# Attention with mixed heads and a dense block: two six-chunk first units, unread products on TensorE, and k and v loaded by head pair

## The chip, the cores and the metric

The kernel runs on one core of one Trainium2 chip. The metric is the device time of one execution in microseconds (us). A profile is one execution taken by the hardware profiler; its span is the time from the first to the last instruction.

## What is computed

Attention over 4 batches, 12 heads, 448 tokens and 64 columns a head, whose heads are mixed before and after the softmax, and behind it a dense block with a token mix of rank 32:

```
scores = scale * matmul(q, k^T)                     # per batch and head
scores = einsum('bhij,hg->bgij', scores, w_pre)     # mix the heads
attn   = softmax(scores, axis=-1)
attn   = einsum('bhij,hg->bgij', attn, w_post)      # mix them again
x      = matmul(attn, v), heads side by side        # (4, 448, 768)
u      = x + (x^T @ U @ V)^T                        # mix the tokens
out    = u + relu(u @ w_ch1) @ w_ch2                # 768 -> 3072 -> 768
```

## The kernel before

A chunk is ten tokens of a batch with all their twelve heads. The tokens of a batch are cut into units of 9 to 12 chunks (table `UNITS`, four units a batch), and each unit goes through the following steps; a step is an entry of a plan, with the engines that may run it, a rank, the steps it needs and the buffers it holds. `Plan.order` writes the order of all steps, engine by engine, from the ranks (table `RANK`) and its own costs. Each engine then runs its list strictly in that order.

- Scores (`qk`, L412 to L419): a head pair p of unit u. Four products of 64 (or 60) rows by 448 columns run beside each other in the four quarters of TensorE's array: two heads, each in two halves of the unit's rows (up to 124 with four leading zero rows). They fill one of four PSUM tiles (`bank`), which ScalarE (ACT) or VectorE (DVE) copies to SBUF (`qk_out`, L433).
- Relay (`relay`, L435 to L437): one DMA a head copies its rows into the tile `t` so that a chunk's token-head pairs lie on partitions. The destination has ten rows. There are twelve relays a unit, issued by SP, those of the first two units by SP or ACT (L454). `t` has two buffers, used by units in turn.
- Premix (`premix`, L457 to L463): two chunks at a time, product of `t` with `wpre`. It needs all twelve relays of its unit. Then the row maximum on DVE (`neg_max`, L469), two exponentials on ACT (`exp`, L474), a reciprocal, and on GpSimd (POOL) the scaled weights `wr` (L484).
- Postmix (`postmix`, L486 to L499): 28 small products; ACT or DVE copies them to the tile `a` (`post_out`).
- Attention times v (`av`, L530 to L547): two steps a unit, three head pairs each, which need the unit's last `post_out`. L539 is the main part, L547 the rest of 64 keys. The results are added up in `acc`, and behind a batch's last unit comes the token mix (`tp`, `t1`, `hp`).

SP issues almost all DMAs in one queue in order: k of a batch in four loads of one or two head pairs (`K_LOADS`), all held until the first premix of the preceding batch's last unit (L410); q of a unit in two loads; v of a batch in one load of 1536 KB (L528); the relays; and weights. Behind the attention, from about 360 us on, the dense block runs in products of 128 x 128 by 448 (L992, L1100), whose operands DVE, ACT and POOL split into two parts (steps `W`, `T`, `w`, `S`).

Of the kernel before, what the change touches and what calls it, by code (L numbers as in the profile page):

```python
# [8 lines left out]
F32 = mybir.dt.float32  # L9
# [12 lines left out]
UNITS = [[10, 12, 12, 11], [11, 12, 12, 10], [12, 12, 12, 9], [11, 12, 12, 10]]  # L22
NG = 4
NJ = 4
# [4 lines left out]
MC = 10  # L29
# [16 lines left out]
class Unit:  # L46


    def __init__(self, b, gi):
        self.b, self.gi, self.n = b, gi, UNITS[b][gi]  # L50
        self.i0 = MC * sum(UNITS[b][:gi])
        self.rows = MC * self.n
        self.tokens = min(S, self.i0 + self.rows) - self.i0

# [3 lines left out]
    e0=-73.073, estep=7.59, er=5.082, qk_lead=5.047, qk_step=0.838, av_off=4.137, av_step=0.959, post=4.408,  # L58
    kr=1.361, vr=0.943, qr=4.83, mx=0.636, ex=1.029, ep=2.968, po=2.763, qo=1.169, uv0=6, uvs=0.013, uv1=2.315,
    raw=5.531, k0=-13.837, kstep=0.705, m0=7.671, pu=1.842, ev=29.543, lead=14.83, t0=-3.828, ts=0.557,  # L60
    t1=2.012, ta=31.914, tb=3.276, dl=32.545, hl=13.674, out=3,
# [6 lines left out]

WEIGHT = {("POOL", "ACT"): 1.0, ("POOL", "DVE"): 3.221, ("DVE", "POOL"): 0.8, ("ACT", "DVE"): 1.3}
# [22 lines left out]
class Plan:  # L92
# [29 lines left out]
    def order(self):  # L122
# [10 lines left out]
        events, seq, now, wire, out, shared, landed = [], 0, 0, 0, [], 0, []  # L133
# [40 lines left out]
        while events:  # L174
# [28 lines left out]
            while moved:  # L203
                moved = False
                for e in free:
# [22 lines left out]
                    if e == "PE" and now - free[e] > 600:  # L228
                        cost += min(cost, 850)
# [22 lines left out]
def build(tc, q2, kt, vj, wpre_in, wpost_in, u_in, v_in, ident, w1j, w2, out, show=None):  # L252
# [115 lines left out]

    units = [Unit(b, gi) for b in range(B) for gi in range(NG)]
    nu = len(units)  # L370
    chunks, first = [], {}
# [9 lines left out]
    load("wpre0", lambda: wpre, wpre_in, -30)  # L381
    load("wpost", lambda: wpost, wpost_in, -12)
# [14 lines left out]
    K_LOADS = ((0, 1), (1, 1), (2, 2), (4, 2))  # L397
    K_AT = (0, 1, 2, 2, 4, 4)
# [798 lines left out]
```

## Time and profile before

| | us |
|---|---|
| median of 3 timed runs (lowest, highest) | 1050.91 (1049.37, 1052.29) |
| the profiled execution | 1047.36 |
| its span | 1045.5 |
| TensorE busy in the span | 1000.9 |
| VectorE, ScalarE, GpSimd busy | 786.8, 473.6, 357.4 |

The engines run beside each other, so only one of them can be full, and busy time is not yet time on the path to the end: a wait counts where it delays the engine that sets the end. "Granted clock" is TensorE's clock as a share of 2.4 GHz; 0.50 is 1.2 GHz. A line ends with the idle time of the engine before it and what ended it, in brackets.

### The profile page before, as it was taken

To read this page: it belongs to the slowest core of one execution; us is meant where nothing else is said; L and a number is where in the kernel's file an instruction comes from. 1 tells how busy PE (TensorE), PEld (TensorE's weight loads), DVE (VectorE), ACT (ScalarE), POOL (GpSimd) and SP (SyncE) were. 2 spreads that over 40 slices of the span, in tenths; PEclk is the share of its full clock that TensorE was granted. 3 is DMA by queue.
4 is the path that set the end of the run, shared out by engine and by line. 5 is a ranking of instruction groups with operands and counts; after the bars stand their busy time and mean duration, and the time that the engine had idled before them with its cause. 6 is when DMAs were issued, how large, how long until landed. Compare 5 with 4: busy or idle time off the path is not lost.

```text
span 1045.5 us, 28572 instructions
## 1 busy us (share of the span) xinstructions
PE 1000.9 (96%) x11908; PEld 840.0 (80%) x11908; DVE 786.8 (75%) x1183; ACT 473.6 (45%) x980; POOL 357.4 (34%) x457
## 2 busy tenths in 40 slices
PE   6899999999899997999999999999999999999998
PEld 2465666666556696898998999999999999999997
DVE  3474575577567788899999897895999999996223
ACT  2677677777777864543433333441333323430000
POOL 3121121112112686765655543450432423322000
PEclk8899999999999999999999999999999999999999
DMA  6764655566585324345444444686353454440023
GB/s 220 208 176 149 203 176 170 180 221 181 182 262 181 97 95 145 108 137 157 148 154 138 140 146 132 191 280 253 94 168 125 138 171 131 151 149 1 1 81 131
DMA packets 84481, 161.30 MB, mean 154 GB/s; under 512 B 8624, under 2 KB 68992, under 8 KB 83840
## 3 DMA queue, kind: packets, MB, share of 16 engines
q1 hardware_dynamic: 82912, 157.11, 46.8%
q10 hardware_dynamic: 1440, 2.37, 0.7%
q8 instruction: 94, 1.54, 0.6%
q14 instruction: 35, 0.29, 0.1%
HBM read 86.13 MB, written 34.60 MB: 115 GB/s over the span
## 4 chain that ended last, share of the span: by engine, by line
PE 77%; DVE 12%; issue 5%; ACT 3%; DMA 2%; POOL 1%; SPq 0%; ACTq 0%; DVEq 0%; POOLq 0%
PE bank L1100 33%; PE bank L992 20%; PE bank L498 6%; PE bank L419 5%; PE bank L539 5%; PE bank L462 5%; DVE aw L686 2%; ACT e L474 1%; PE bank L547 1%; DVE aw L687 1%; DVE aw L682 1%; DVE w L341 1%; DVE x L691 1%; DVE st L469 1%; DVE x L692 1%
## 5 line engine op out<-in xcount | busy, mean ns | idle before, releaser
L1100 PE MATMUL bank<-u,w 128*128 128x448 f32 x1728 | 345.9, 362 | 0.0
L1100 PEld LDWEIGHTS bank<-u,w 128*128 128x128 f32 x1728 | 324.0, 187 | 21.6
L992 PE MATMUL bank<-u,w 128*128 128x448 f32 x1512 | 307.0, 363 | 4.8 <-DVE hs L1005 2.9
L992 PEld LDWEIGHTS bank<-u,w 128*128 128x128 f32 x1512 | 283.6, 188 | 26.1 <-ACT bank L334 2.6
L1103 DVE TENSOR_TENSOR acc<-acc,bank 128x896 f32<-128x896 f32 (+1 forms) x99 | 104.2, 1053 | 78.6 <-PE bank L1100 75.9
L696 POOL TENSOR_TENSOR aw<-aw,x 128x384 f32<-128x384 f32 x74 | 83.8, 1132 | 201.1 <-DVE x L692 197.4
L498 PEld LDWEIGHTS bank<-wr,e 60*64 60x64 f32 x5040 | 92.4, 136 | 52.4 <-issue 33.7
L469 DVE TENSOR_REDUCE st<-bank 128x2 f32<-128x896 f32 x90 | 97.4, 1086 | 45.6 <-PE bank L462 35.6
L474 ACT ACTIVATE e<-bank,st 128x448 f32<-128x448 f32 x180 | 113.0, 639 | 24.7 <-DVE st L469 9.8
L341 POOL TENSOR_TENSOR w<-aw,w 128x384 fp32r<-128x384 f32 x84 | 97.7, 1171 | 67.5 <-ACT w L334 66.0
L334 ACT CAST w<-aw 128x384 fp32r<-128x384 f32 x103 | 52.4, 515 | 134.9 <-PE bank L1100 65.9
L498 PE MATMUL bank<-wr,e 60*64 60x60 f32 x5040 | 95.7, 221 | 14.3 <-issue 9.3
L675 ACT ACTIVATE x<-kr 128x384 f32<-128x384 f32 (+1 forms) x80 | 44.3, 554 | 133.6 <-DMA kr<-in_w 101.2
L419 PE MATMUL bank<-k,q 64*64 64x448 f32 (+1 forms) x768 | 93.4, 569 | 8.0 <-DMA k<-in_kt 5.0
L462 PE MATMUL bank<-t,wpre 64*64 64x448 f32 x720 | 89.5, 569 | 6.4 <-DMA t<-acc 4.8
L477 POOL TENSOR_SCALAR st<-st 128x2 f32<-128x2 f32 x90 | 18.6, 206 | 205.2 <-ACT e L474 203.7
L334 ACT COPY hs<-bank 128x448 f32<-128x448 f32 x88 | 46.9, 533 | 76.2 <-PE bank L992 74.9
L1060 DVE SCALAR_TENSOR_TENSOR u<-hs,u 128x448 fp32r<-128x448 f32 x96 | 73.9, 800 | 0.0
L687 DVE SCALAR_TENSOR_TENSOR aw<-x,aw 128x384 f32<-128x384 f32 x88 | 67.3, 765 | 6.7
L334 ACT COPY a<-bank 128x840 f32<-128x840 f32 (+1 forms) x64 | 54.5, 854 | 34.6 <-PE bank L498 34.2
L692 DVE SCALAR_TENSOR_TENSOR x<-kr,x 128x384 f32<-128x384 uint32 (+2 forms) x99 | 66.8, 675 | 3.4
L334 ACT COPY s<-bank 124x896 f32<-124x896 f32 x64 | 58.1, 912 | 20.6 <-PE bank L419 14.5
(69 smaller groups left out, 1016.6 us busy)
## 6 DMA issues: line engine op xcount, KB each, us to landing
hd<-hs SPq DMA_DIRECT2D x96, 224.0 KB
hs<-hd SPq DMA_DIRECT2D x96, 224.0 KB
t<-s SPq DMA_DIRECT2D x99, 210.0 KB
kr<-in_w1j SPq DMA_DIRECT2D x48, 384.0 KB
kr<-in_w SPq DMA_DIRECT2D x48, 384.0 KB
t<-s SPq DMA_DIRECT2D x36, 192.5 KB
v<-in_vj SPq DMA_DIRECT2D x4, 1536.0 KB
q<-in_q SPq DMA_DIRECT2D x32, 186.0 KB
```

Source lines behind the costliest of these rows:

```text
L334: eng.copy(out=o, in_=i)
L341: eng.tensor_tensor(out=o, in0=a, in1=b, op=ALU.subtract)
L419: eng.matmul(o[at, i, :S], lhsT=q[d, p, at], rhs=k[d, p, :], start=True, stop=True)
L462: eng.matmul(o[64 * j:64 * j + 64, i, :S], lhsT=wpre[64 * i:min(64 * i + 64, QW)], rhs=tt[u % 2][64 * i:min(64 * i + 64, QW), n, :], start ...
L469: eng.tensor_reduce(out=mx, in_=T["pre", k][:, :, :S], axis=AX.X, op=ALU.max, negate=True)
L474: eng.activation(out=e[:, i], in_=T["pre", k][:, i, :S], func=ACTF.Exp, bias=T["mx", k][:, i:i + 1], accum_out=sm[:, i:i + 1])
L498: eng.matmul(d, lhsT=e[64 * j:64 * j + HALF, i, x * KB:x * KB + KB], rhs=wr[64 * j:64 * j + HALF, i].rearrange("p (g m) -> p g m", m=MH), ...
L687: eng.scalar_tensor_tensor(out=f32(a), in0=f32(x), scalar=MIN_NORMAL, in1=f32(a), op0=ALU.is_ge, op1=ALU.mult)
L696: eng.tensor_tensor(out=f32(a), in0=f32(a), in1=f32(x), op=ALU.add)
L992: eng.matmul(o, lhsT=w[:, x, i * 128:(i + 1) * 128], rhs=u[:, i, y, :], start=j < 2 and i + t == 0, stop=i + t == 4, skip_group_check=True)
L1100: eng.matmul(ps[:, j, :S], lhsT=w[:, x, cc * 128:(cc + 1) * 128], rhs=h, start=(i == 0), stop=(i == len(todo) - 1))
L1103: eng.tensor_tensor(out=two(b, c, n), in0=two(b, c, n), in1=T.pop(("dn", g, b, c))[:, :n, :S], op=ADD)
```

## The change

Batch 0 is cut into five units of 6, 6, 12, 12 and 9 chunks. A unit of six chunks has at most 64 rows with its zero rows, so one `qk` step takes two head pairs, one in each half of the array's columns; its copy has 128 rows, and it is followed by four relays of six chunks. The relays of the first unit alone may be issued by ACT. TensorE gets two steps `warm`, three and five products of a zeroed tile into a PSUM tile that nobody reads, the second behind the scores of both small units. The k of batch 0 comes in three loads of two head pairs, that of the others in six of one, held from some twenty chunks ahead of the batch; v comes in six loads. The planner's own cost for a cold TensorE and the ranks are changed, which moves steps on all engines.

```diff
-UNITS = [[10, 12, 12, 11], [11, 12, 12, 10], [12, 12, 12, 9], [11, 12, 12, 10]]
+UNITS = [[6, 6, 12, 12, 9], [11, 12, 12, 10], [12, 12, 12, 9], [11, 12, 12, 10]]
...
+        self.pairs = 2 if self.rows + QA <= 64 else 1
+        self.cols = 64 if self.pairs == 2 else QW
...
-    e0=-73.073, estep=7.59, er=5.082, qk_lead=5.047, qk_step=0.838, av_off=4.137, av_step=0.959, post=4.408,
+    e0=-97.289, estep=7.59, er=4.323, qk_lead=4.915, qk_step=0.84, av_off=3.794, av_step=0.935, post=4.408,
...
+SHARED = 1
+WARM = 3, 5
...
-    K_LOADS = ((0, 1), (1, 1), (2, 2), (4, 2))
-    K_AT = (0, 1, 2, 2, 4, 4)
+    K_LOADS = ((0, 2), (2, 2), (4, 2)), tuple((p, 1) for p in range(H // 2))
+    Q_LOADS = ((0, 2), (2, 4)), ((0, 6),), ((0, 3), (3, 3))
...
     for b in range(B):
-        for p, n in K_LOADS:
-            plan.add(("k", b, p), [("SP", (450, 650 * n))], partial(load_k, b=b, p=p, n=n), rank_qk(b * NG, 2 * p) - RANK["kr"], [("premix", first[b * NG - 1] // 2)] if b else (), [("k", b)])
+        start = first[of_batch[b][0]]
+        for p, n in K_LOADS[b > 0]:
+            plan.add(("k", b, p), [("SP", (450, 650 * n))], partial(load_k, b=b, p=p, n=n), rank_qk(of_batch[b][0], 2 * p) - RANK["kr"], [("premix", (start - 20 + p) // 2)] if b else (), [("k", b)])
...
         for j in range(2):
-            at = slice(64 * j, min(64 * j + 64, QW))
+            at = of = slice(64 * j, min(64 * j + 64, QW))
+            pj = p
+            if units[u].pairs == 2:
+                at, of, pj = slice(64 * j, 64 * j + 64), slice(0, 64), p + j
             for i in range(2):
                 d = slice(i * D, (i + 1) * D)
-                eng.matmul(o[at, i, :S], lhsT=q[d, p, at], rhs=k[d, p, :], start=True, stop=True)
+                eng.matmul(o[at, i, :S], lhsT=q[d, pj, of], rhs=k[d, pj, :], start=True, stop=True)
...
-                plan.add(("relay", u, h), [("SP", cost)] + [("ACT", cost)] * (u < 2), partial(relay, u=u, h=h), r + RANK["qo"], [("qk_out", u, p)], s + [("t", u)])
+                plan.add(("relay", u, h), [("SP", cost)] + [("ACT", cost)] * (u < SHARED), partial(relay, u=u, h=h), r + RANK["qo"], [("qk_out", u, p)], s + [("t", u)])
...
+    def blank():
+        return sb["xn"].tile([JP, NJ, LW], F32R, "xh", ("xn", "blank")).bitcast(F32).rearrange("p j n -> p (j n)")
+
+    def warm(eng, i, n):
+        z, o = blank(), bank("pre", ("warm", i))
+        for _ in range(n):
+            eng.matmul(o[:64, 0, :S], lhsT=z[:, S:S + 64], rhs=z[:, :S], start=True, stop=True)
+
+    plan.add("blank", [("DVE", 700)], lambda eng: eng.memset(blank(), 0.0), -30, (), [("xn", "blank")])
+    for i, n in enumerate(WARM):
+        plan.add(("warm", i), [("PE", 760 * n)], partial(warm, i=i, n=n), (-30, -1)[i], ["blank"] + [[], [("qk", 1, 4), ("qk", 0, 4)]][i], [("pre", ("warm", i)), ("xn", "blank")])
...
-            plan.add(("v", un.b), [("SP", (500, 3900))], partial(load_v, b=un.b), rank_av(u, 0) - RANK["vr"], [("premix", first[u] // 2)], [("vr", un.b)])
+            for p in range(H // 2):
+                plan.add(("v", un.b, p), [("SP", (450, 650))], partial(load_v, b=un.b, p=p), rank_av(u, p // AV * AV) - RANK["vr"], [("premix", (max(first[u], first[u + 1] - 6) + p) // 2)], [("vr", un.b)])
```

The order of three places follows, first before and then after. A row is a line of the program, the operation, what it writes and reads, its shape and a count; L419 and L435 are scores, L462 and L495 premixes, L498 and L531 postmixes, L437 and L456 relays.

**TensorE, from the last scores of the second unit to the first postmix** (bank0 to bank3 are the PSUM tiles, q_1 and q_2 the q of the second and third unit):

```order
L419 MATMUL bank3_61<-k_0_151,q_1_159 64x448 x2
L419 MATMUL bank3_61<-k_0_151,q_1_159 60x448 x2
L462 MATMUL bank0_58<-t0_142,wpre_141 64x448 x4
L462 MATMUL bank1_59<-t0_142,wpre_141 64x448 x4
L462 MATMUL bank2_60<-t0_142,wpre_141 64x448 x4
L462 MATMUL bank3_61<-t0_142,wpre_141 64x448 x4
L498 MATMUL bank0_58<-wr_0_284,e_0_270 64x12x5 x24
```

```order
L484 MATMUL bank0_58<-xh_0_149 64x448 x3
L435 MATMUL bank1_59<-k_0_153,q_0_147 64x448 x4
L435 MATMUL bank2_60<-k_0_153,q_0_147 64x448 x4
L435 MATMUL bank3_61<-k_0_153,q_0_147 64x448 x4
L435 MATMUL bank0_58<-k_0_153,q_1_158 64x448 x4
L435 MATMUL bank1_59<-k_0_153,q_1_158 64x448 x4
L435 MATMUL bank2_60<-k_0_153,q_1_158 64x448 x4
L484 MATMUL bank3_61<-xh_0_149 64x448 x5
L495 MATMUL bank0_58<-t1_143,wpre_141 64x448 x4
L495 MATMUL bank1_59<-t1_143,wpre_141 64x448 x4
L495 MATMUL bank2_60<-t1_143,wpre_141 64x448 x4
L435 MATMUL bank3_61<-k_0_153,q_2_230 64x448 x2
```

Before, twelve score steps and four premixes stand ahead of the first postmix; now it is three unread products, six score steps, five unread products, three premixes and two score steps of the third unit, of which the first row is shown.

**SP, its first DMAs** (in_q, in_kt are inputs in DRAM; t_142 and t_143 the two relay buffers; acc and s the copies of the scores):

```order
L379 DMA wpre<-in_wpre 124x64
L406 DMA q_149<-in_q 128x372
L402 DMA k_151<-in_kt 128x448
...
L402 DMA k_151<-in_kt 128x896
L379 DMA wpost<-in_wpost 128x60
...
L406 DMA q_159<-in_q 128x372 x2
L437 DMA t_142<-acc 10x10x448 x6
L437 DMA t_143<-acc 10x12x448 x3
L437 DMA t_143<-s_234 10x12x448
...
L406 DMA q_260<-in_q 128x372
...
L528 DMA v_282<-in_vj 128x3072
```

```order
L418 DMA q_147<-in_q 128x4x64
L414 DMA k_153<-in_kt 128x896
L418 DMA q_158<-in_q 128x6x64
...
L389 DMA wpre<-in_wpre 124x64
...
L389 DMA wpost<-in_wpost 128x60
L456 DMA t_143<-acc 10x6x448 x6
L456 DMA t_142<-acc 10x6x448 x7
L418 DMA q_230<-in_q 128x372 x2
L456 DMA t_142<-acc 10x6x448 x5
L561 DMA v_300<-in_vj 128x512
L456 DMA t_143<-acc 10x12x448 x6
```

Before, SP has half the relays of both first units; now it has six of the first and all twelve of the second, with the third unit's q between them, and one sixth of v ahead of the third unit's relays.

**TensorE, around the first scores of batch 1** (k_1128 and k_1012 are that batch's k):

```order
L462 MATMUL bank_60<-t_143,wpre 64x448 x4
L462 MATMUL bank_58<-t_143,wpre 64x448 x4
L462 MATMUL bank_59<-t_143,wpre 64x448 x4
L498 MATMUL bank_61<-wr_284,e_270 64x12x5 x24
...
L419 MATMUL bank_60<-k_1128,q_159 64x448 x2
...
L419 MATMUL bank_58<-k_1128,q_159 64x448 x2
```

```order
L435 MATMUL bank_58<-k_1012,q_230 64x448 x2
...
L495 MATMUL bank_61<-t_142,wpre 64x448 x4
L531 MATMUL bank_60<-wr_346,e_259 64x12x5 x24
...
L435 MATMUL bank_59<-k_1012,q_230 64x448 x2
...
L495 MATMUL bank_58<-t_142,wpre 64x448 x4
L435 MATMUL bank_60<-k_1012,q_230 64x448 x2
...
L531 MATMUL bank_59<-wr_256,e_239 64x12x5 x24
```

Before, three premixes in a row go ahead of the new batch's scores, three of which then follow each other with no premix between them; now scores, premixes and postmixes alternate.

## Rows read from the trace of the kernel before

**Rows 1.** The page's first part: TensorE's busy time, share of the span, instructions.

```profile
PE 1000.9 (96%) x11908; PEld 840.0 (80%) x11908; DVE 786.8 (75%) x1183; ACT 473.6 (45%) x980; POOL 357.4 (34%) x457
```

**Rows 2.** Stretches: length, each engine's busy time, granted clock, DMA share, GB/s.

```profile
5.00:9.00 4.00, 3.39 (x20) 0.71 (x16) 0.00 (x0) 1.31 (x2) 4.00 (x2) 1.00 0.95 311
12.00:20.00 8.00, 5.25 (x56) 1.59 (x48) 5.52 (x6) 2.72 (x3) 0.00 (x0) 1.00 0.64 217
22.00:23.00 1.00, 0.99 (x8) 0.53 (x12) 0.00 (x0) 0.00 (x0) 0.00 (x0) 0.50 0.64 220
85.60:89.00 3.40, 3.40 (x36) 1.38 (x40) 0.17 (x1) 1.79 (x3) 0.52 (x2) 0.50 0.24 70
400.00:420.00 20.00, 13.65 (x59) 11.02 (x58) 16.59 (x23) 9.06 (x19) 14.05 (x13) 0.91 0.43 143
```

**Rows 3.** TensorE in order of time: start, length, instructions, idle time before.

```profile
4.38 1.77 PE L419 MATMUL bank<-k,q 64*64 64x448 f32 x8 [4.38 <-DMA k<-in_kt]
...
22.01 5.98 PE L462 MATMUL bank<-t,wpre 64*64 64x448 f32 x32 [4.76 <-DMA t<-acc]
30.45 3.00 PE L498 MATMUL bank<-wr,e 60*64 60x60 f32 x112 [2.46 <-POOL wr L484]
...
39.97 0.69 PE L498 MATMUL bank<-wr,e 60*64 60x60 f32 x32 [2.56 <-issue]
...
85.51 3.21 PE L419 MATMUL bank<-k,q 64*64 64x448 f32 x16 [0.70 <-ACT e L474]
```

**Rows 4.** TensorE up to 45.36 us, by line: L419, L462, L498 (records in brackets).

```profile
0.00:45.36 45.36, 15.73 (x120) 0.85 0.71 216
...
0.00:45.36 45.36, 10.47 (x56) 0.85 0.71 216
...
0.00:45.36 45.36, 6.09 (x280) 0.85 0.71 216
```

**Rows 5.** TensorE in order of time at full clock: premix, postmix, scores.

```profile
57.60 0.93 PE L462 MATMUL bank<-t,wpre 64*64 64x448 f32 x8
58.35 0.99 PE L498 MATMUL bank<-wr,e 60*64 60x60 f32 x56
59.17 0.93 PE L419 MATMUL bank<-k,q 64*64 64x448 f32 x8
```

**Rows 6.** SP and ScalarE in order of time: first k, first relays, first exponential.

```profile
1.59 0.43 SPq L402 DMA_DIRECT2D k<-in_kt  x1
...
7.14 13.36 SPq L437 DMA_DIRECT2D t<-acc  x9
...
28.10 0.63 ACT L474 ACTIVATE e<-bank,st 128x448 f32<-128x448 f32 x1 [9.36 <-DMA t<-s]
```

**Rows 7.** Issue of relays on SP, ns (least/median/most): up to 30 us, then from 45.

```profile
L437 SPq DMA_DIRECT2D t<-acc x9: 755/1222/1555, 7.1 to 19.2; - x9
...
L437 SPq DMA_DIRECT2D t<-s x163: 755/756/1482, 45.0 to 346.9; - x163
```

**Rows 8.** Attention times v in order of time: units of 12 and of 9 chunks.

```profile
179.99 2.07 PE L539 MATMUL bank<-a,v 128*64 128x120 f32 x36
181.99 0.58 PE L547 MATMUL bank<-a,v 64*64 64x60 f32 x24
...
292.35 1.62 PE L539 MATMUL bank<-a,v 128*64 128x90 f32 x36 [0.56 <-DVE a L336]
293.89 0.56 PE L547 MATMUL bank<-a,v 64*64 64x45 f32 x24
```

**Rows 9.** Who TensorE waited for, 45 to 380 us: total, times, longest.

```profile
PE bank L498 <- issue: 6.8, 8, 1.4
PE bank L419 <- ACT e L474: 2.2, 5, 0.7
...
PE bank L462 <- ACT e L474: 0.6, 2, 0.4
...
PE bank L462 <- DMA t<-s: 0.5, 1, 0.5
```

More of the change, by code (lines that the diff above doesn't have):

```diff
@@ L132, in order @@
         ready = {e: [] for e in free}
-        events, seq, now, wire, out, shared, landed = [], 0, 0, 0, [], 0, []
+        events, seq, now, wire, out, shared, landed, cold = [], 0, 0, 0, [], 0, [], 4500
         def push(k, t):
@@ L367, in OUT, with side @@
         return [("ACT", 55 + 0.833 * n), ("DVE", 75 + 1.042 * n)]
-    units = [Unit(b, gi) for b in range(B) for gi in range(NG)]
+    units = [Unit(b, gi) for b in range(B) for gi in range(len(UNITS[b]))]
     nu = len(units)
+    of_batch = [[u for u in range(nu) if units[u].b == b] for b in range(B)]
+    def side(u):
+        return (nu - 1 - u) % 2 ^ 1
     chunks, first = [], {}
@@ L439, in build @@
+        r = QA + 64 * (h // 2 - p)
+        eng.dma_start(out=tt[side(u)][QA + h::H][:, :n], in_=T["s", u, p][r:r + MC * n, h % 2])
     at = 0
     for u, un in enumerate(units):
-        b, size = un.b, 128 * (H // 2) * QW
+        b, size = un.b, 128 * (H // 2) * un.cols
         src = q2[at:at + size].rearrange("(p h i) -> p h i", p=128, h=H // 2)
         at += size
-        for p in range(0, H // 2, 3):
-            plan.add(("q", u, p), [("SP", (430, 600))], partial(load_q, u=u, p=p, n=3, src=src), rank_qk(u, 2 * p) - RANK["qr"], [("premix", first[u - 2] // 2)] if u > 1 else (), [("q", u)])
@@ L446, in build @@
-        for p in range(H // 2):
+        at_q, hold = [], [("qk", 0, 4)] if u == 1 else []
+        for p, n in Q_LOADS[min(u, 2)]:
+            at_q += [p] * n
+            plan.add(("q", u, p), [("SP", (430, 200 * n * un.cols // QW))], partial(load_q, u=u, p=p, n=n, src=src), rank_qk(u, 2 * p) - RANK["qr"], [("premix", first[u - 2] // 2)] if u > 1 else (), [("q", u)])
+        for p in range(0, H // 2, un.pairs):
             r = rank_qk(u, 2 * p)
             o, s = ("qk", (u, p)), [("s", (u, p))] if lent(u, p) is None else []
-            plan.add(("qk", u, p), [("PE", 760)], partial(qk, u=u, p=p), r, [("q", u, p // 3 * 3), ("k", b, K_AT[p])],
+            plan.add(("qk", u, p), [("PE", 760)], partial(qk, u=u, p=p), r, [("q", u, at_q[p]), *hold, *{("k", b, x) for x in (([p // 2 * 2]) if b == 0 else range(p, p + 1))}],
@@ L794, in build @@
     for b in range(B):
-        RB = first[(b + 1) * NG] + RANK["uv0"]
-        us = range(b * NG, (b + 1) * NG)
+        us = of_batch[b]
+        RB = first[us[-1] + 1] + RANK["uv0"]
         for k in range(KC // 2):
@@ L1144, in lay_out @@
     for b in range(B):
-        for gi in range(NG):
+        for gi in range(len(UNITS[b])):
             un = Unit(b, gi)
-            part = np.zeros((2, D, H // 2, QW), q.dtype)
+            part = np.zeros((2, D, H // 2, un.cols), q.dtype)
             for n in range(un.n):
```

53 lines of the change are left out of this document (29 added, 24 removed).

## Prediction

> **What bounds the kernel now.** I read the page first: TensorE is busy for 1000.9 of 1045.5 us [rows 1], so a change can win only where TensorE waits or runs at the lower of its two clocks. Next came the stretches and TensorE's order in time. From about 45 us on it hardly stops; before that it does. The first scores start at 4.38 us, the first premix at 22.01, the first postmix at 30.45, and at 39.97 another wait of 2.56 us ends [rows 3]. The clock adds to it: granted 0.50 (1.2 GHz) at 22 us after the long wait [rows 2], and the very first head pair took 1.77 us where one takes 0.93 later [rows 3, 5], as at half clock, though the record reads 1.00 there [rows 2].
>
> How much is lost there? By 45.36 us TensorE had done 15 head pairs of scores (120 records of 8 a pair), 7 premixes (56 of 8) and 5 postmixes (280 of 56) [rows 4]. At full clock a premix starts 0.75 us before what follows it, a postmix 0.82, and a head pair lasts as long as a premix [rows 5]. That is 22 x 0.75 + 5 x 0.82 = 20.6 us of work in 45.4 us: **24.8 us lost**, the largest loss in the program.
>
> What sets it is the way of the scores: product, copy out of PSUM, relay by DMA into the layout the premix reads. A unit's premix needs all twelve relays. While relays alone move, the core moves 217 GB/s at a DMA share of 0.64; while the first loads move it is 311 GB/s at 0.95 [rows 2]. ScalarE's relays also hold up its exponentials: the first starts at 28.10, 9.36 us after ScalarE's last work, and 2.35 us before the first postmix [rows 6, 3].
>
> **The change, part by part.** *First premix.* A unit of six chunks has 60 rows, so two head pairs fill one product group: three groups, copies and 12 relays of 105 KB, where before 12 of 175 KB shared the queues with unit 1's. The three unread products start at about 1.8 us (a memset on VectorE first, an estimate) and at half clock take 1.5 us each (twice 0.75), to 6.3; the first k and q land at about 5.5 (the first pair's k landed 2.8 us after its issue began, at 4.38 [rows 3, 6], and this load is 224 KB larger, 0.7 us at 311 GB/s [rows 2]). So they cost the first group some 0.8 us. The last k, with 1.8 MB ahead of it, lands near 9.4, and the third group ends at 10.2. Relays begin 2.76 us behind the first product (7.14 against 4.38 [rows 6, 3]), at 9.0; SP and ScalarE issue six each. An issue took 1.22 us when both queues were full and 0.756 alone [rows 7]; I take 0.9, so the last is out at 14.4 and lands at 16.5. Unit 1's groups end at 12.5, five unread products (3.75 us) cover the wait to 16.3, and the first premix starts at **16.5** at full clock, 5.5 us earlier than now.
>
> *What is late next.* SP now issues all relays of unit 1, with unit 2's q behind the seventh: 14.4 + 12 x 0.77 + 2 x 0.45 = 24.5. That q lands near 22, and in TensorE's order two head pairs of unit 2 stand ahead of the first postmix. TensorE is through with three premixes at 18.8 and waits 3.2 us; I charge a fall of the clock, 1.7 us, as in the 3.4 us at 0.50 behind the waits before 85.51 [rows 2, 3]. Unit 2's 12 relays of 215 KB follow at 217 GB/s, 0.99 us each, and v's first load: 24.5 + 0.45 + 11.9 = 36.9, landed 2.4 later. So unit 2's premix starts at **39.3**. TensorE's own work would allow 38.9 (from 22.0: nine head pairs, three premixes and six postmixes, 13.9; the clock, 1.7; and some 1.3 of waiting for exponentials, an estimate). By then it has done 15 head pairs, 6 premixes and 6 postmixes, 20.7 us, and lost 18.6: **6.2 us gained** (24.8 - 18.6). Its ends: if bytes alone bind, 5.2 MB of relays at 217 GB/s from 9.4 us take 24.0, and 0.64 MB of q and v, spread over all engines of which relays keep 0.64 busy, 1.9 more; landed 2.4 later that is 37.7, 7.8 gained. If every issue takes 1.22, 14.4 + 24 x 1.22 + 3 x 0.45 + 2.4 = 47.5, 2.0 lost. I take the value near 0.756, the row of 163 relays with SP alone [rows 7].
>
> The share of 0.64 is near ten of sixteen engines. The Trainium skill (DMA: Bandwidth & Descriptors, Why a DMA increments its semaphore by 16 and not by 1) says a transfer runs on the largest number of engines up to 16 that divides the slowest dimension of both sides, here ten rows. By that rule relays of six chunks run no wider, and the trace agrees; on sixteen engines unit 2's relays would be bound by issue alone and land near 36.5.
>
> *Unit 3.* Between unit 2's relays and the last of unit 3's, SP has five loads of v, three of q and one of U. With 2.0 MB of those counted as above, the relays' engines need 11.9 + 5.9 us, landed by 57.1; TensorE reaches that premix at 39.3 + 12 x 0.75 + 4 x 0.82 + 4 x 1.66 (attention steps of 60 columns, below) = 58.2. The margin of 1.1 is thinner than the errors behind it: **0.7 lost** (0 to 2).
>
> *Fifth unit.* Batch 0 keeps 45 chunks, 24 score groups and 450 rows, but attends to v in 10 steps, not 8. The main part costs 2.00 us at 120 columns and 1.54 at 90, so 0.16 without columns; the rest takes 0.58 and 0.56 and hardly falls [rows 8]. **1.5 us added** for two steps (0.3 if the rest shrank with its columns, 3.3 if a main part never fell below 1.54).
>
> The Trainium skill (TensorEngine Tiling, Instruction Overhead) puts a fixed cost of about 60 cycles on a matmul, so that one column takes as long as 60; this speaks against halving the columns. By it the 1.5 stands, by plain proportion it would be 0.3; the rest's 0.58 and 0.56 agree with the rule.
>
> *k and v by head pair.* The k of a batch was loaded when its predecessor's last unit began, and its scores stood in a bunch behind a row of premixes; now six loads come some ten chunks earlier and scores alternate with premixes throughout. From 45 to 380 us scores and premixes waited 2.2 + 0.6 us for ScalarE and 0.5 for a relay [rows 9], most of it at the batch boundaries, and the wait that ends at 85.51 was followed by 3.4 us at half clock, 1.7 lost [rows 3, 2]. I take all of it, **5.0 won** (0 to 5.0). The seven more DMA issues a batch lie in SP's slack: a unit's 12 relays and two q take 10 us of some 19. The 6.8 us of postmix waits on "issue" [rows 9] have no cause that I can see; unchanged.
>
> *Dense part.* Order is the same but for one or two steps moved; the stall at 400 to 420 us, 6.35 us without a product [rows 2], stays: 0, within 2 either way.
>
> **Sum:** -6.2 + 0.7 + 1.5 - 5.0 = -9.0 us. The profiled execution took 1047.36 us, so 1038.4; the median of the timed runs is 1050.91, 3.55 above it, and there the change gives **1041.9**.
>
> **Rivals.** *The boundary waits stay* because they belong to ScalarE's queue (2.8 of the 3.3 us name it), not to late k: then only the head counts, 1046.9. For it: ScalarE's work is as long as before. Against it: the bunch of scores in the order is gone. 0.20.
>
> *More is won:* relays at the speed of their bytes (7.8), no loss in unit 3, 5.0 at the boundaries and 2 in the dense part: -7.8 + 1.5 - 5.0 - 2 = -13.3, so 1037.6. For it: nothing but bytes must bind SP. Against it: 163 relays alone never went under 0.755 [rows 7]. 0.12.
>
> *The unread products do not do their work:* they use a quarter of the array, and if the clock stays low behind them, the groups and the five products take double, and the first premix slips by about 2.5 us: 1044.4. For it: nothing in this trace shows such products. 0.08.
>
> *Slower: SP as the only issuer.* Place: SP's queue from 14 to 60 us. If a relay's issue costs 1.22 us there, as SP's did in the head [rows 7], unit 2's premix comes at 47.5 (2.0 lost), unit 3's 0.7 late, k, in the same queue, stays late and the boundaries win nothing: +2.0 + 0.7 + 1.5 = +4.2, 1055.1. It decides from about 1.1 us an issue. Against it: that 1.22 was measured with both queues full. 0.06.
>
> **Numbers.** Forecast 0.50; the four rivals 0.46; 0.04 for no change by small losses together. About 0.3% (3.2 us) is what a measurement of this kernel tells from no change, so faster means under 1047.8: forecast, the win, the unread products and two thirds of the first rival, 0.83; same 0.11; slower 0.06. The range 1036 to 1048 leaves out the slower case, the no-change case and the far parts of two others, under 0.2.
>
> **What would show it.** Right: first premix near 16.5, unit 2's near 39, the granted clock 1.00 from about 8 to 19 us, relays on SP near 0.8 us, no wait of scores for ScalarE at the batch boundaries, ten attention steps in batch 0. Wrong: a first premix after 19, unit 2's after 43, products of 1.5 us beyond 10 us, the boundary waits of the same size, or a longer stall after 390 us.

## The result, and the profile after

The changed kernel took **1040.0 us** (median of 6 runs, 1039.07 to 1045.45) beside 1050.92 us for the kernel before, a ratio of 0.9909 with a 95% interval of 0.9883 to 0.9936. In the experiments the same kernel was timed again, with 0.9933 [0.9907, 0.9959]. The forecast of 1041.9 and its range hold; that the terms behind it hold does not follow, and half of them did not. The sum came out by luck, as shown below.

The two profiled executions are closer together than the medians: 1047.36 and 1043.51 us, 3.85 us apart, where the medians are 10.9 apart. Runs of one kernel spread over 10 us and more here (the kernel before: 1044 to 1057 over four series), so a pair of profiles says which wait stands where, and only the medians say what a part is worth.

The page's first part for the changed kernel, beside [rows 1]:

```profile
PE 1002.3 (96%) x12044; PEld 840.2 (81%) x12044; DVE 790.3 (76%) x1194; ACT 467.5 (45%) x970; POOL 356.4 (34%) x461
```

TensorE in order of time, with the columns of [rows 3] (L484 are the unread products, L435 scores, L495 premix, L531 postmix, L572 and L580 attention times v):

```profile
6.65 1.34 PE L435 MATMUL bank<-k,q 64*64 64x448 f32 x8
8.51 4.26 PE L435 MATMUL bank<-k,q 64*64 64x448 f32 x40 [0.53 <-DMA k<-in_kt]
12.71 3.97 PE L484 MATMUL bank<-xh 112*64 112x448 f32 x10
18.78 2.49 PE L495 MATMUL bank<-t,wpre 64*64 64x448 f32 x24 [2.10 <-DMA t<-acc]
23.75 2.59 PE L435 MATMUL bank<-k,q 64*64 64x448 f32 x16 [2.48 <-DMA q<-in_q]
26.10 1.72 PE L531 MATMUL bank<-wr,e 60*64 60x60 f32 x56
...
43.80 2.17 PE L495 MATMUL bank<-t,wpre 64*64 64x448 f32 x16 [2.59 <-DMA v<-in_vj]
...
49.42 1.26 PE L572 MATMUL bank<-a,v 128*64 128x60 f32 x36
50.62 0.55 PE L580 MATMUL bank<-a,v 64*64 64x30 f32 x24
50.99 0.96 PE L495 MATMUL bank<-t,wpre 64*64 64x448 f32 x8
...
58.83 0.56 PE L531 MATMUL bank<-wr,e 60*64 60x60 f32 x18 [1.52 <-issue]
```

The first premix comes 3.2 us earlier than before and runs at full clock (24 matmuls in 2.49 us). Then unit 2 is late twice: its scores wait for q until 23.75, and its premix for its relays until 43.80. The kernel before began its seventh premix at 42.95, 0.85 us earlier than the changed kernel, with two postmixes (1.6 us) fewer done. So at that point most of the start's lead is gone.

SP's queue over the same stretch, and the stretches (columns as in [rows 2]):

```profile
8.99 12.09 SPq L456 DMA_DIRECT2D t<-acc  x13
21.12 0.95 SPq L418 DMA_DIRECT2D q<-in_q  x2
...
26.18 0.48 SPq L561 DMA_DIRECT2D v<-in_vj  x1
...
32.81 5.29 SPq L456 DMA_DIRECT2D t<-s  x6
38.14 1.47 SPq L561 DMA_DIRECT2D v<-in_vj  x2
```

```profile
24.00:28.00 4.00, 4.00 (x76) 2.40 (x72) 0.06 (x2) 2.58 (x6) 0.39 (x1) 0.57 0.56 161
...
36.00:44.00 8.00, 5.33 (x196) 3.70 (x200) 1.68 (x4) 4.86 (x9) 1.18 (x5) 1.00 0.86 250
44.00:51.00 7.00, 7.00 (x146) 4.59 (x142) 3.02 (x6) 4.15 (x10) 1.05 (x4) 0.76 0.84 268
```

SP issues a relay in 0.93 us (13 in 12.09, with a pause of 1.3 us in it) and later 0.88, near what the sum assumed. The last of unit 2 is out at 38.10, yet its premix starts 5.7 us later, with the DMA engines at a share of 0.86. The bracket of that premix names a load of v, which a premix does not need. It is the relay that came late: by the semaphore records of the trace it landed at 43.67, and the twelve relays of the unit landed 1.18 us apart (30.64 to 43.67), where the sum had 0.99. The clock falls behind both waits (0.57 from 24 to 28 us, 0.76 from 44 to 51).

Who TensorE waited for from 45 to 380 us, beside [rows 9]:

```profile
PE bank L531 <- issue: 5.9, 8, 1.6
PE bank L495 <- ACT e L507: 2.1, 2, 1.3
PE bank L435 <- DVE s L342: 1.9, 1, 1.9
```

Scores no longer wait for ScalarE's exponentials (2.2 us in five waits before); premixes do instead, 2.1 us in two, where they had 0.6. The one wait of a premix for a relay is gone, and a new wait of 1.9 us stands at the second batch boundary. Added up without "issue", scores and premixes wait 5.6 us here and 3.5 in the second profile, where the two profiles of the kernel before have 4.5 and 4.6: other waits have come in place of those that went.

### The profile page after: what moved, and what is told of

Its sections match the earlier page's. It is cut to its first block, busy times and chain, and to the rows that moved or that the text cites. A ratio compares the mean times of both kernels' runs of the same rounds, so it can differ in the third digit from the quotient of the medians.

```text
span 1041.7 us, 28885 instructions
## 1 busy us (share of the span) xinstructions
PE 1002.3 (96%) x12044; PEld 840.2 (81%) x12044; DVE 790.3 (76%) x1194; ACT 467.5 (45%) x970; POOL 356.4 (34%) x461
## 4 chain that ended last, share of the span: by engine, by line
PE 58%; DVE 4%; ACT 0%; issue 0%; ACTq 0%; DVEq 0%
PE bank L1134 33%; PE bank L1026 25%; DVE aw L720 1%; DVE aw L721 0%; DVE acc L875 0%; DVE x L726 0%; DVE u L347 0%; DVE aw L875 0%; DVE aw L716 0%; DVE x L725 0%; DVE hs L1039 0%; DVE acc L822 0%; DVE w L347 0%; DVE hs L342 0%; DVE xl L347 0%
## 5 line engine op out<-in xcount | busy, mean ns | idle before, releaser
L531 PEld LDWEIGHTS bank<-wr,e 60*64 60x64 f32 x5040 | 91.1, 136 | 44.3 <-issue 30.6
L709 ACT ACTIVATE x<-kr 128x384 f32<-128x384 f32 x82 | 45.6, 556 | 127.2 <-DMA kr<-in_w 99.1
L531 PE MATMUL bank<-wr,e 60*64 60x60 f32 x5040 | 94.1, 220 | 8.2 <-issue 5.9
L435 PE MATMUL bank<-k,q 64*64 64x448 f32 (+1 forms) x768 | 92.9, 549 | 5.8 <-DMA q<-in_q 2.5
L495 PE MATMUL bank<-t,wpre 64*64 64x448 f32 x720 | 86.8, 546 | 8.6 <-DMA v<-in_vj 2.6
L1094 DVE SCALAR_TENSOR_TENSOR u<-hs,u 128x448 fp32r<-128x448 f32 x96 | 78.9, 852 | 0.0
L340 ACT COPY a<-bank 128x840 f32<-128x840 f32 (+1 forms) x72 | 60.5, 845 | 35.2 <-PE bank L531 35.2
L572 PEld LDWEIGHTS bank<-a,v 128*64 128x64 f32 x1224 | 57.4, 139 | 13.5 <-ACT a L340 4.2
L726 DVE SCALAR_TENSOR_TENSOR x<-kr,x 128x384 f32<-128x384 uint32 (+2 forms) x99 | 64.1, 647 | 3.4
```

Of the source, the lines that this page charges most:

```text
L340: eng.copy(out=o, in_=i)
L435: eng.matmul(o[at, i, :S], lhsT=q[d, pj, of], rhs=k[d, pj, :], start=True, stop=True)
L495: eng.matmul(o[64 * j:64 * j + 64, i, :S], lhsT=wpre[64 * i:min(64 * i + 64, QW)], rhs=tt[side(u)][64 * i:min(64 * i + 64, QW), n, :], sta ...
L531: eng.matmul(d, lhsT=e[64 * j:64 * j + HALF, i, x * KB:x * KB + KB], rhs=wr[64 * j:64 * j + HALF, i].rearrange("p (g m) -> p g m", m=MH), ...
L1094: eng.scalar_tensor_tensor(out=h[:, 1, :], in0=T["hr", f, b], scalar=0.0, in1=f32(h[:, 0, :]), op0=ALU.max, op1=ALU.subtract)
```

## The experiments

All are timed in five rounds beside the kernel before on the same chip, except where the text says otherwise. There are four series: again, nowarm, oldunits and oldk; newk, oldranks and plain; oldv, vlate and sv; headonly. The medians of the kernel before in them are 1050.13, 1049.50, 1050.02 and 1049.45 us. A comparison across series goes by the ratios.

| kernel | what it is | median, us | ratio to the kernel before, 95% interval |
|---|---|---|---|
| again | the changed kernel | 1043.45 | 0.9933 [0.9907, 0.9959] |
| nowarm | without the unread products | 1040.12 | 0.9905 [0.9875, 0.9935] |
| oldunits | batch 0 in four units | 1041.14 | 0.9921 [0.9890, 0.9951] |
| plain | without both head parts | 1039.62 | 0.9894 [0.9864, 0.9924] |
| headonly | with only the head parts | 1051.06 | 1.0020 [0.9992, 1.0048] |
| newk | the kernel before, with early k | 1045.87 | 0.9958 [0.9939, 0.9978] |
| oldk | k loaded as before | 1054.15 | 1.0031 [1.0008, 1.0055] |
| oldv | v loaded as before | 1047.32 | 0.9987 [0.9957, 1.0016] |
| oldranks | ranks of the kernel before | 1046.68 | 0.9979 [0.9955, 1.0003] |
| vlate | batch 0's v behind unit 2's relays | 1046.47 | 0.9976 [0.9948, 1.0004] |
| sv | vlate, ScalarE issues relays too | 1050.33 | 1.0010 [0.9986, 1.0034] |

**The changed kernel again.**

> The changed kernel once more, for a second profiled execution. First theory (the sum on record: the head gives 6.2 us, the batch boundaries 5.0): the medians stand 9 to 11 us apart as before, and a second profile shows unit 2's premix starting near 39 us. Rival (the head gives back nearly all it won, because unit 2's Q and V arrive late): unit 2's premix starts again at 43 to 44 us, within 1 us of the first profile, and no more than 2 us of the gain are there at that point.

The time comes out as before within the interval. The second profile has the first premix at 18.46 and unit 2's at:

```profile
43.18 2.76 PE L495 MATMUL bank<-t,wpre 64*64 64x448 f32 x16 [2.80 <-DMA v<-in_vj]
```

The rival holds: the start does not keep its lead.

**The unread products taken out.**

```
-        for _ in range(n):
+        for _ in range(0):
             eng.matmul(o[:64, 0, :S], lhsT=z[:, S:S + 64], rhs=z[:, :S], start=True, stop=True)
```

> The changed kernel without the unread products (sixteen matmuls in two groups); every other instruction and every order stays. First theory (they hold TensorE's clock while it waits): a fall of the clock of about 3.4 us at half speed, so 1.7 us of work, comes in ahead of or at the first premix, once or twice: 1.7 to 3.4 us slower, 1041.7 to 1043.5. Rival (the clock falls anyway at 24 and 44 us, and the stretch before the first premix waits for relays): within 1 us of the changed kernel.

TensorE in order of time, and the stretch of the first premixes:

```profile
6.28 6.99 PE L435 MATMUL bank<-k,q 64*64 64x448 f32 x48 [6.28 <-DMA k<-in_kt]
19.10 4.76 PE L495 MATMUL bank<-t,wpre 64*64 64x448 f32 x24 [5.83 <-DMA t<-acc]
23.61 2.00 PE L435 MATMUL bank<-k,q 64*64 64x448 f32 x16
```

```profile
18.00:24.00 6.00, 4.90 (x28) 1.76 (x32) 2.20 (x3) 1.79 (x5) 0.19 (x1) 0.50 0.60 181
```

Without the products the clock falls, and three premixes take 4.76 us where they take 2.49 with them. The products do what they were put there for. It is worth nothing: the scores after these premixes stand behind q, which lands near 23.7 us either way, so 2.3 us faster premixes become a 2.48 us wait. The time does not go up (1040.12).

**Batch 0 in its old units.**

```
-UNITS = [[6, 6, 12, 12, 9], [11, 12, 12, 10], [12, 12, 12, 9], [11, 12, 12, 10]]
+UNITS = [[10, 12, 12, 11], [11, 12, 12, 10], [12, 12, 12, 9], [11, 12, 12, 10]]
```

> The changed kernel with batch 0's units as before (10, 12, 12 and 11 chunks, no unit whose head pairs share the array); the early K, the unread products and the ranks stay. First theory (two units of six chunks are worth 6.2 us in the head and cost 0.7 and 1.5 later): about 4 us slower, near 1044. Rival (the head hands its gain back at unit 2): within 1 us, or up to 1.5 us faster, since two extra attention steps go.

The rival again: 1041.14, no different from the changed kernel.

**Both head parts taken out.** The two edits above together.

> The changed kernel without both of its head parts: batch 0's units as before and no unread products; the loads of K and V by head pair and the ranks stay. First theory (head worth 6.2 less 2.2 later): 4 to 6 us slower than the changed kernel, 1044 to 1047. Rival (the head gives nothing): within 1.5 us of it, 1039 to 1043.

1039.62 us, the lowest median of all, though not apart from the changed kernel's within the intervals. It is the simpler kernel: it keeps the loads and the ranks, and with them the relays of the second unit on SP alone and the planner's new costs.

**Only the head parts.** The two units of six chunks and the unread products stay; k, v and the ranks are put back by the edits of oldk, oldv and oldranks below.

> The changed kernel with only its head kept: two units of six chunks whose head pairs share the array, and the unread products; K and V of batches 1 to 3 are loaded as before (V of batch 0 too), and the ranks are those of the kernel before. First theory (the sum on record: 6.2 us in the head, less 0.7 and 1.5): about 4 us under the kernel before, 1045 to 1047. Rival, after the other runs (the head gives its gain back by unit 2): within 2.5 us of the kernel before on either side, 1047.5 to 1052.5.

1.0020 [0.9992, 1.0048]: between 0.8 us faster and 5.0 slower. Its trace shows the same give-back:

```profile
19.13 2.49 PE L496 MATMUL bank<-t,wpre 64*64 64x448 f32 x24 [2.63 <-DMA t<-acc]
...
43.02 3.24 PE L496 MATMUL bank<-t,wpre 64*64 64x448 f32 x32 [0.15 <-ACT s L340]
```

Four kernels of different make (nowarm, oldunits, plain, headonly) agree that the head gains nothing that these intervals, some 3 us to either side, can show.

**Early k alone, in the kernel before.**

```
-    K_LOADS = ((0, 1), (1, 1), (2, 2), (4, 2))
+    K_LOADS = ((0, 1), (1, 1), (2, 2), (4, 2)), tuple((p, 1) for p in range(H // 2))
...
-        for p, n in K_LOADS:
-            plan.add(("k", b, p), [("SP", (450, 650 * n))], partial(load_k, b=b, p=p, n=n), rank_qk(b * NG, 2 * p) - RANK["kr"], [("premix", first[b * NG - 1] // 2)] if b else (), [("k", b)])
+        for p, n in K_LOADS[b > 0]:
+            plan.add(("k", b, p), [("SP", (450, 650 * n))], partial(load_k, b=b, p=p, n=n), rank_qk(b * NG, 2 * p) - RANK["kr"], [("premix", (first[b * NG] - 20 + p) // 2)] if b else (), [("k", b)])
```

> The kernel before with one part of the change alone: K of batches 1 to 3 in loads of one head pair, each let go some twenty chunks ahead of its batch; units, ranks, V, and the head stay as before. First theory (the batch boundaries are worth about 5.0 us by the sum on record, the head the rest): about 5 us under the kernel before, near 1045. Rival, after the first runs (the early K is the whole gain; the head gives nothing): 8 to 11 us under the kernel before, 1039 to 1042.

4.4 us under the kernel before (1050 x 0.0042; interval 2.3 to 6.4). The first theory's 5.0 is in it, the rival's 8 to 11 is not. Its one profile (1050.23 us, the second slowest of its runs) does not show where: scores no longer wait for exponentials, but for VectorE's copies, and premixes wait more. From 45 to 380 us, beside [rows 9]:

```profile
PE bank L419 <- DVE s L336: 3.0, 2, 2.0
PE bank L462 <- ACT e L474: 2.3, 2, 1.9
```

**k as before, in the changed kernel.**

```
-    K_LOADS = ((0, 2), (2, 2), (4, 2)), tuple((p, 1) for p in range(H // 2))
+    K_LOADS = ((0, 2), (2, 2), (4, 2)), ((0, 1), (1, 1), (2, 2), (4, 2))
...
-            plan.add(("k", b, p), [("SP", (450, 650 * n))], partial(load_k, b=b, p=p, n=n), rank_qk(of_batch[b][0], 2 * p) - RANK["kr"], [("premix", (start - 20 + p) // 2)] if b else (), [("k", b)])
+            plan.add(("k", b, p), [("SP", (450, 650 * n))], partial(load_k, b=b, p=p, n=n), rank_qk(of_batch[b][0], 2 * p) - RANK["kr"], [("premix", first[of_batch[b - 1][-1]] // 2)] if b else (), [("k", b)])
```

> The changed kernel with the K of batches 1 to 3 loaded as before: four loads a batch of one, one, two and two head pairs, held until the last unit of the batch before has had its first premix. First theory (the waits at the batch boundaries belonged to the late K): the waits of TensorE around 85, 170 and 290 us return, with the clock's fall at 86: 4 to 6 us slower, near 1045. Rival (they belonged to ScalarE's queue of exps, or the new ranks keep them away): within 1 us of the changed kernel.

Far more than either said: 1054.15, some 11 us over the changed kernel of the same series and over the kernel before as well. TensorE at the third batch boundary, and that stretch:

```profile
277.26 1.76 PE L532 MATMUL bank<-wr,e 60*64 60x60 f32 x56 [2.80 <-ACT s L340]
...
279.89 1.77 PE L436 MATMUL bank<-k,q 64*64 64x448 f32 x8 [0.86 <-ACT s L340]
281.59 3.05 PE L573 MATMUL bank<-a,v 128*64 128x120 f32 x36
```

```profile
277.00:285.00 8.00, 6.87 (x128) 5.16 (x132) 1.20 (x2) 3.17 (x7) 0.58 (x2) 0.58 0.62 202
```

A postmix waits for ScalarE's copy of scores, 2.80 us; then the clock is at 0.58, and an attention step that takes 2.07 us takes 3.05. SP issues the batch's four k loads at 261 to 264 us here. In the changed kernel five of the six are issued from 245.81 to 251.86. The scores stand in a bunch again, and ScalarE's queue does not copy them at that pace. So the wait bears ScalarE's name and comes with k: from 45 to 380 us scores and premixes wait 12.2 us here, against 5.6 and 3.5 in the changed kernel. Not all of the 11 us is k's in this one profile: 4.2 to 4.8 us more than in the changed kernel were lost by 55 us (table below), ahead of the first load that the edit moves.

**v as before.**

```
-            for p in range(H // 2):
-                plan.add(("v", un.b, p), [("SP", (450, 650))], partial(load_v, b=un.b, p=p), rank_av(u, p // AV * AV) - RANK["vr"], [("premix", (max(first[u], first[u + 1] - 6) + p) // 2)], [("vr", un.b)])
+            plan.add(("v", un.b), [("SP", (500, 3900))], partial(load_v, b=un.b), rank_av(u, 0) - RANK["vr"], [("premix", first[u] // 2)], [("vr", un.b)])
```

> The changed kernel with V in one load a batch again, let go at the first premix of the batch's first unit. First theory (V by head pair only spreads the same bytes, so the early K is what the boundaries gained): within 1.5 us of the changed kernel. Rival (V's 1.5 MB in one piece holds up the relays behind it in SP's queue and on the wires, at each of four batches): 3 to 6 us slower, and unit 2's premix starts over 2 us later.

1047.32, some 4 to 7 us over the changed kernel's medians: the rival's size. Unit 2's premix starts at 49.31, over 2 us later as the rival said, but the order has attention steps ahead of it, and TensorE has lost no more by 55 us (23.0, against 25.1 and 24.5 in the changed kernel). So its one profiled execution, 1043.93 us and among its fastest runs, does not show where the time goes.

**The old ranks.** The whole table RANK is that of the kernel before; its first line for both, and nothing else changes.

```
-    e0=-97.289, estep=7.59, er=4.323, qk_lead=4.915, qk_step=0.84, av_off=3.794, av_step=0.935, post=4.408,
+    e0=-73.073, estep=7.59, er=5.082, qk_lead=5.047, qk_step=0.838, av_off=4.137, av_step=0.959, post=4.408,
```

> The changed kernel with the table of ranks of the kernel before; units, loads and unread products stay. First theory (the ranks only place what the loads allow): within 1.5 us of the changed kernel. Rival (part of the gain is the new ranks, which fit fewer waits in at the boundaries): 2 to 5 us slower, 1042 to 1046.

1046.68, so the table is worth some 3 to 7 us against the two series of the changed kernel: the rival's size. Its place is not the batch boundaries (table below). One wait in the dense part looks like a piece of it. TensorE's waits there in the kernel before, in the changed one again, and with only the head parts (whose ranks are the old ones):

```profile
496.10 61.48 PE L992 MATMUL bank<-u,w 128*128 128x448 f32 x306 [0.65 <-ACT bank L334]
...
559.19 6.04 PE L992 MATMUL bank<-u,w 128*128 128x448 f32 x29 [1.61 <-DVE hs L1005]
```

```profile
467.59 86.65 PE L1026 MATMUL bank<-u,w 128*128 128x448 f32 x432 [0.81 <-ACT bank L340]
...
554.46 45.85 PE L1026 MATMUL bank<-u,w 128*128 128x448 f32 x228 [0.21 <-DVE hs L1039]
```

```profile
521.24 79.07 PE L1026 MATMUL bank<-u,w 128*128 128x448 f32 x394 [1.03 <-ACT bank L340]
```

It is not. Added up, these waits are 2.26 us before (2.25 in a second profile), 1.02 in the changed kernel, 1.03 in headonly and 1.09 in oldranks: with either table of ranks the same. Where the 3 to 7 us stand is open.

**Batch 0's v held back.**

```
-                plan.add(("v", un.b, p), [("SP", (450, 650))], partial(load_v, b=un.b, p=p), rank_av(u, p // AV * AV) - RANK["vr"], [("premix", (max(first[u], first[u + 1] - 6) + p) // 2)], [("vr", un.b)])
+                plan.add(("v", un.b, p), [("SP", (450, 650))], partial(load_v, b=un.b, p=p), rank_av(u, p // AV * AV) - RANK["vr"], [("premix", (max(first[u], first[u + 1] - 6) + p) // 2)] + [("relay", 2, 11)] * (un.b == 0), [("vr", un.b)])
```

> The changed kernel with one thing held back: batch 0's six loads of V wait until the last relay of unit 2 has been issued. First theory (between 20 and 44 us the relays wait for bandwidth, and V's 1.5 MB in that stretch is what makes unit 2 late): unit 2's premix starts 1.5 to 3 us earlier, at 41 to 42 us, and the whole is 0 to 3 us faster, less what the first attention steps then wait. Rival (the relays' issue on SP's queue is the bound, 0.84 us a relay): unit 2's premix starts within 0.7 us of 43.2 to 43.8, and the time stays within 1.5 us.

TensorE, and the stretch:

```profile
42.42 1.74 PE L495 MATMUL bank<-t,wpre 64*64 64x448 f32 x16 [1.83 <-DMA q<-in_q]
...
59.63 0.90 PE L531 MATMUL bank<-wr,e 60*64 60x60 f32 x19 [3.64 <-issue]
```

```profile
36.00:44.00 8.00, 6.08 (x172) 3.58 (x165) 2.70 (x4) 4.32 (x8) 0.74 (x3) 1.00 0.70 232
```

Unit 2's premix starts 0.8 to 1.4 us earlier, with the DMA share at 0.70 in place of 0.86: v is a part of that lateness, less than the 1.5 to 3 us expected, and not the whole. (The bracket names q; the last relay landed at 42.18, and the twelve landed 1.12 us apart with no v among them.) The kernel as a whole became slower, 1046.47, which the theory did not foresee. v then moves from 43 us on (the share from 44 to 60 is 0.85), and one wait on "issue" in that stretch is 3.64 us where the changed kernel has 1.52 at the same place. Behind it the clock is at 0.50 from 59.6 to 64.0 us. From the 7th to the 21st postmix this profile loses 12.3 us, those of the changed kernel 6.6 and 5.3, about as much as the medians lie apart.

**ScalarE issues relays too.** The edit above, and

```
-SHARED = 1
+SHARED = 3
```

> As the kernel with V held back, and the relays of units 1 and 2 may go through ScalarE's queue too, every other one. Rival of the run before (SP's issue is the bound): unit 2's relays are out in half the time, and its premix starts 3 us or more earlier than with V held back alone, near 38 to 39 us. First theory (the transfers themselves are the bound): it starts within 1 us of that kernel, and ScalarE's exps, which stand behind the relays in its queue, come later: 0 to 3 us slower in all.

Neither came out. Unit 2's premix starts at 45.86, 3.4 us later than with v held back alone, and the time is 1050.33. The first relay of the unit is issued at 30.32, where vlate has 26.65, and the last seven that SP issues in this stretch, three of unit 2 and four of unit 3, stand wide apart:

```profile
34.22 12.03 SPq L456 DMA_DIRECT2D t<-s  x7
```

So this run does not compare the two with the same start. What it does show of the bound is the pace: with two queues the twelve relays of unit 2 are out within 8.7 us (30.32 to 39.02), 11 of them follow the first at 0.66 us each, and they land 1.03 us apart (33.62 to 44.93). SP's issue is not the bound there; the transfers are.

**The kernel before, profiled a second time** (one execution, 1044.01 us).

> The kernel before once more, for a second profiled execution, since the first one was the fastest of its runs. First theory: unit 2's premix starts again at about 39 us with the same waits ahead of it (4.8, 2.5 and 4.4 us). Rival: the waits in the head differ by over 2 us from one execution to the next, so that a gain of 6 us there can't be read from one pair.

The 39 us in that expectation is the forecast for the changed kernel and was put there by mistake; what compares is the seventh premix, at 41.98 here and 42.95 in the first profile. The waits of 4.8 (relays), 4.6 (k; 4.4) and 2.3 us (POOL; 2.5) returned, so the heads differ by about 1 us there. The larger difference between the two profiles is at the first batch boundary. The first profile, beside the row at 85.51 in [rows 3], and then the second:

```profile
83.69 0.34 PE L498 MATMUL bank<-wr,e 60*64 60x60 f32 x8 [1.20 <-issue]
```

```profile
81.33 0.34 PE L498 MATMUL bank<-wr,e 60*64 60x60 f32 x8 [0.65 <-issue]
...
83.15 1.78 PE L419 MATMUL bank<-k,q 64*64 64x448 f32 x16 [0.70 <-ACT e L474]
```

```profile
78.00:90.00 12.00, 10.65 (x268) 6.39 (x263) 6.01 (x11) 8.48 (x21) 2.70 (x9) 1.00 0.46 153
```

The same two waits, one of them 0.55 us shorter: the clock stayed at 1.00, and sixteen scores took 1.78 us, not 3.21. So the fall of the clock that the prediction charged to this boundary is not there in every execution.

## Where TensorE loses its time, over all traces

From each trace I took the start of every step of TensorE and subtracted the full-clock length of all steps ahead of it (a premix 0.75 us, a postmix 0.81, attention by its columns); what is left is lost. The table gives what was lost in three stretches of time, one profile each.

| kernel | 0 to 55 us | 255 to 300 us | 300 to 365 us |
|---|---|---|---|
| before, twice | 25.1, 23.3 | 8.4, 8.6 | 8.7, 9.5 |
| headonly | 23.3 | 10.8 | 7.5 |
| newk | 27.4 | 7.5 | 9.9 |
| oldranks | 23.4 | 6.5 | 11.0 |
| oldk | 29.3 | 10.2 | 7.3 |
| the changed kernel, twice | 25.1, 24.5 | 6.8, 6.6 | 6.7, 8.6 |
| nowarm | 24.4 | 6.7 | 6.2 |
| plain | 20.4 | 5.6 | 6.3 |

The head of the changed kernel loses what the kernel before loses. At the third batch boundary the four traces with late k lose 9.5 us on average, all ten with early k 6.8 (oldunits, oldv, vlate and sv, not in the table, 7.7, 5.0, 6.3, 9.3). In the last units the five traces with the old ranks lose 9.3, the nine with the new ones 7.3 (the same four: 8.8, 6.7, 6.9, 8.2). These are 2.7 and 2.0 us, and single traces spread by more than 2.

The 2.7 cannot be laid to k alone: three of the four traces with late k have the old ranks as well. Counted over the same work, from the 53rd postmix to the 76th, newk and oldranks (early k, old ranks) lose 13.2 and 15.0 us, no less than the kernel before with 13.3 and 12.9; oldk, late k with the new ranks, loses 15.6, and the eight traces with early k and the new ranks 11.4 on average (9.0 to 14.4; the changed kernel 10.7 twice). So a gain shows there only where both are new. Behind the last attention step, with 0.20 us for a product of the dense block, the kernel before loses 12.6 and 12.7 us to the end, the changed kernel 12.2 and 12.1, headonly and oldranks 10.7 and 11.0: 0.5 us gained, and not by the ranks. The two profiled executions of the kernel before and the two of the changed one lie 2.7 us apart on average, so the 7 to 11 us of the medians are not all in these traces.

## Why the prediction was right, and where it was not

*The first premix: 16.5 said, 18.8 and 18.5 measured.* Relays began at 8.99 (9.0 said), unit 1's scores ended at 12.7 (12.5 said), and the issue cost was as assumed. The step that failed is "the last is out at 14.4 and lands at 16.5": ScalarE's sixth relay was out at 15.0 and landed 3.2 us later, at 18.2, and the premix started 3.7 us behind the issue, not 2.1.

*Unit 2's premix: 39.3 said, 43.8 and 43.2 measured.* The last relay was out at 38.1 (36.9 said). The failed step is again the landing, "landed 2.4 later": 5.7 us, with q and v in the same stretch at a share of 0.86. vlate shows v's part, about 1 us. Most of the rest is the relays' own pace: they landed 1.18 us apart and 1.12 without v, where the sum took 0.99 for each and so let them land as fast as they were issued. q's part I did not test apart. By 43.80 the changed kernel had done the 20.7 us of the prediction and so lost 23.1, not 18.6: **1.7 us gained where the sum had 6.2**, and 2.3 in the second profile. The second profile of the kernel before is 1.0 us earlier there, and headonly's time says the whole head is worth -0.8 to +5.0 us. The term of -6.2, with its +0.7 and +1.5, came to -4.0; measured, 2.1 on the other side, with no gain over 0.8 in the interval.

*The fifth unit: right.* A step at 60 columns takes 1.57 us (49.42 to 50.99), 1.66 was said. Ten steps against eight make 4 x 1.57 + 2 x 1.92 - 2 x 2.09 - 2 x 2.24 = 1.5 us (steps of 90, 100 and 110 columns; four of 120 are in both), 1.5 said. *Unit 3:* no premix of it waits for a relay; 0.7 was not lost.

*k by head pair: right in size,* 4.4 us alone [2.3, 6.4] against 5.0; *the mechanism is shown in part.* Waits of scores for exponentials are 2.2 us in both profiles of the kernel before and in headonly and 1.5 in oldk, and none in newk, oldranks, nowarm, plain and both profiles of the changed kernel. But the sum took them as won, and other waits came in their place; in newk, where k is the only change, no trace shows the 4.4 us. That the waits named ScalarE made me give "they belong to ScalarE's queue" 0.20; oldk shows ScalarE's name on waits that k's loads bring. The 1.7 us in it for the clock at 85 us rested on one execution, and in a second one it is not there.

*The dense part: right,* 0.5 us less lost behind the last attention step, 0 within 2 said.

*The unread products: rival refuted in its cause, but they are worth nothing.* They hold the clock and shorten the premixes by 2.3 us, and q takes it back. (By the row at 12.71 they use 112 x 64 of the array, not "a quarter".) I had written "TensorE is through with three premixes at 18.8 and waits 3.2 us" and did not draw the conclusion.

*What the sum had no term for.* From newk (-4.4) to plain (-11.1, 8.0 to 14.3) lie v by head pair, the new ranks, batch 0's own loads, the second unit's relays on SP alone and the planner's new costs: 6 to 7 us. v and the ranks have runs of their own; the other three have none. I had counted the ranks as "one or two steps moved" and v as slack in SP's queue. So an overrated head of about 6 us stood against an unseen gain of about 6, and the sum came out by luck. The parts do not add: taking back k, v or the ranks from the changed kernel costs 11 to 14, 4 to 7 and 3 to 7 us by the medians, more than the whole gain. An order is made for its loads.

*SP as the only issuer:* 0.84 to 0.93 us a relay with the pauses between them, and the longest single issue before 60 us took 1.14, not 1.22; the rival did not come.

*Open:* where in the run newk gains its 4.4 us and where oldv and oldranks lose what their medians show. Each has one profile, and these spread as widely as the differences. For vlate the one profile has a place, the 3.64 us wait and the half clock behind it.

## What to carry to other kernels

Follow a gain at the start to the first point where both kernels have done the same work: here a lead of 3.2 us at the first premix was handed back at unit 2's q and relays, which neither the small units nor the warm clock brought sooner. Put the landing of a DMA in a busy stretch at what the trace shows in a busy stretch (4 to 6 us behind its issue here), not at the latency of a quiet one, and look how far apart a row of transfers lands, not only how fast it is issued. And read a wait's name as the last to come, not as the cause: where scores stood in a bunch, it was the load that held them, and a retuned order is a part of the change with its own price.

## What the runs showed of the hardware that was not expected

**Waits on "issue" are late blocks of instructions.** The fourteen traces have 159 waits of TensorE on "issue" of some 0.15 us or more in their first 380 us. Counted over everything that the trace records of TensorE (weight loads, products, semaphore waits), 155 of them stand at the same place in a period of exactly 256 instructions. In the changed kernel they stand ahead of product 850, 977, 4138, 4389 and 8060, among others, in the kernel before ahead of 344, 1228, 1480, 2112 and 4138, in nowarm, which has 16 products fewer, again ahead of 977 and 4138. And 157 of the 159 end 1.2 to 1.8 us after a packet of 16,384 bytes has landed in the trace's instruction queue. The Trainium skill (Runtime: NRT & Kernel Launch, Instruction fetch mechanics) says that an engine's instructions are fetched in blocks of 256, and that crossing from one to the next is mostly hidden. The traces agree with the block. The crossing is not hidden here: 5 to 16 waits a profile, of 0.2 to 4.3 us each, 3.1 us in all (oldk) to 14.4 (oldunits). The longest, in oldunits:

```profile
37.77 1.02 PE L531 MATMUL bank<-wr,e 60*64 60x60 f32 x28 [4.34 <-issue]
```

It stands ahead of product 345, where plain waits 0.36; the stretch from 32 to 36 us has a DMA share of 1.00. The border at product 850 cost 1.52 and 1.44 us in two executions of the changed kernel, under 0.3 in nowarm and 3.64 in vlate, where v was on its way. So the place is fixed by the program and the length by the execution; that the data DMAs make a block late is likely from these rows, not shown. In the prediction these 6.8 us [rows 9] had "no cause that I can see".

**Nearly the same waits, with and without a fall of the clock.** At the first batch boundary 1.20 + 0.70 us of waits were followed by 3.4 us at 0.50, and 0.65 + 0.70 us by none, in one and the same program.

**The same DMAs landed 4 us later in another execution.** In oldk SP's order up to 74 us is the changed kernel's, and the twelve relays of unit 2 were issued at the same times (the last out at 38.40, against 38.10). They landed by 48.00 in place of 43.67, and the premix came at 48.13 in place of 43.80:

```profile
38.87 3.26 PE L436 MATMUL bank<-k,q 64*64 64x448 f32 x16 [1.50 <-DMA q<-in_q]
...
48.13 3.26 PE L496 MATMUL bank<-t,wpre 64*64 64x448 f32 x16 [2.40 <-DMA t<-s]
```

The waits bring the clock down as well: sixteen scores and two premixes take 3.26 us each, at half clock. I take the 10 us between runs of one kernel to come from such differences; that was not tested.
